# All four pairs of batch 0 with fp32 scores, two heads as row tiles of one step

## The chip, the cores and the metric

The kernel runs on one core of a Trainium2 chip. The metric is the device time of one execution in microseconds (us). Five engines work side by side, each through its own instruction list in order: TensorE (PE, matrix products; its weight loads are shown as PEld), VectorE (DVE), ScalarE (ACT), GpSimd (POOL) and SyncE (SP), which issues the DMAs here. They wait for each other through semaphores.

## The reference

Rotary attention over q, k and v of shape 4 x 8 x 576 x 64 (batch, heads, sequence, head dimension) and then an MLP over all 2304 tokens, everything in fp32:

```
q_rot, k_rot = rotate(q), rotate(k)          # x1*cos - x2*sin, x1*sin + x2*cos
scores = q_rot @ k_rot^T / sqrt(64)
attn = exp(scores - max); attn = attn / (sum(attn) + 1e-9)
x = (attn @ v) as (2304, 512)
h = x @ w_in                                 # 512 x 2048
g = s * relu(h)**2 + b
out = g @ w_out                              # 2048 x 512
```

## The kernel before

The 32 heads are 16 pairs; pairs 0 to 3 are batch 0. A pair's 2 x 576 query rows are nine score tiles of 128 rows by 576 keys: tiles 0, 1, 4, 5 belong to the first head and 2, 3, 6, 7 to the second, and tile 8 holds the last 64 rows of both heads, one above the other. Each tile runs through TensorE (`s_tile`, into one of two score buffers of two PSUM banks each), VectorE (`s_max`: scale and row minimum, in place, L652), ScalarE (`s_exp`, L388) and a normalisation that writes p as two f16 parts (`p_a`, `p_b`, into one of five buffers `pab`), then a transposing DMA (L710) and the product with v (`pv_sum`, L731).

Scores come in two ways. The pairs in `FQ`, (0, 1) here, keep q and k in fp32: after the rotation `qk_T` transposes both on TensorE by products with the identity (L739 and L742), `qk_ev` copies the result to SBUF, and `s_tile` multiplies over the 64 rows of one head (L633 and L634, in the profile each fp32 product is two passes). All other pairs split q and k into two f16 parts (`qk_hi`, `qk_lo` into `nat`), transpose them by DMA (L592), keep a copy of k with its halves swapped (`swap_k`, L601), and `s_tile` makes four f16 products over 128 rows per tile (L645 and L646). For these pairs, among the first four, `x_gram` also makes products of q and k with themselves (L537), which give the scale of the split.

Beside the attention of batch 0 the weights are loaded, rebuilt from their two words (`w_sign`, `w_low`, `w_rebias`, `w_join`), squared for their scale (`w_gram`, L456) and, for the first 256 tokens of batch 0 ("unit 0"), used in fp32 (`mlp_in0` L880, `mlp_out0` L897). All later units use weights and activations in two f16 parts (L854, L921).

No loop sets the order of the work: `plan()` lists all pieces with what they read and write, and three tables written out by hand order give the rest. `ORDER` is the order in which the pieces are issued, two letters a piece, `PICKS` the engine of each piece that can run on more than one, and `SLOTS` the buffer that each piece takes. Buffer counts are in `BUFS`. All DMAs go out on SP's queue in the order of `ORDER`.

Of the kernel before, what the change touches and what calls it, by code (L numbers as in the profile page):

```python
# [33 lines left out]
BUFS = {"s": 2, "bank": 2, "po": 1, "nat": 1, "ot": 1, "xc": 4, "xt": 1, "hr": 2, "k": 2, "q": 2, "v": 4, "z": 2, "p": 4, "pab": 5, "pt": 2, "x": 4,  # L34
        "xa": 2, "g": 3, "v16": 4, "qkT": 4, "kS": 4, "vS": 7, "dg": 2}
# [3 lines left out]
    "DTDUAAEAADD_EBEDDcDdDeDfDgAFEODhEPAEAGAHDiECELDjEEDkDlEFA3AJALEMENAIJ1EGEHEIEJEKA4AKA6J2A9DrAdDqAMA5A7DpEREQESETANAeEUJt"  # L39
    "JuJvAgAfDsDtD1AOAPDuD2DVDWDvDwJ3AQATJ4DxDXEaBAAhD3A-ARDYDZJ5DyEbA_EXJwASBBAWEcEeEdJxEmDzEfAwAyDaEgEhD0DbEpAYAxEnAzDmA0Ei"  # L40
    "AXEqD6EVAqArEWE2EjAUD7AZAaErEkElEoD4D5BCJ_KRA8KAJyAtD8EyE1BEAjDnE4KBEsKSBDKTAsEuJ6BHE5AVJzKZAbA1AmJ0LPEtEvAuJ7BGKaKCAlKb"
    "FDAkFEDoLQBRAnBSBFFABIKDAvA2J8KHAoBUAiBTEwKIBXKcBZBVBaKEKJKFD9BrBYKKBtExApD-BsFFBuKLBJKjEzBxBzKdBvBbKMKGBKFQFPBeKUKVKkAc"
    "KeB0ByBNBMKlKNB1BLLRKmBOLSKnE0KOLTKoJ9FSJ-FTK9KrBhBgKpK-KsLUKtKqKuKWKPBkBlFBBfLVBiBPLZBmK_KQBnKvBQLaFdBoFCKXK1BwB2BWBcEY"
    "E3KwKYLALbB4B7KfCSB-FrB6B5B3K2LcBdE6K3FeBpLHBjLzB8FfKgKhKxLdCUCVL0CBBqK4LIB_LJKyLeCTCAc3CCCLACLfLBLKK5CMCWLLABLWLMClLhKz"
    "LiL1LCCNKiLNLDK0L9B9bmbnblboCDCYCmLjCOK6MlCoLkL-CPCbCnL_FuK7LlLmCpMAEZCELnL2L3MBMmFRLOCsLXMJbpCabqCtCvCyLoLgMnLYc4c5Mobr"
    "E7MKMGCzE8c6E9c7E-MpC0L4C1E_CZCcc8MLL5C2MCc9FICuFGC_bwLrLpbyCFLqDCDALsFaMDCwMHbvMIc-FbCXbxbzMMCdFJCeLtLuDBbsMXCGMNFHDDLv"
    "MRb0K8LEb7b5LFb8MUCfGEGFLGCiCILwCHMYLxMSCgMVFpGHFsMZMWMOMPCJGRChCjL6Lyb6btMxL7MuMqb9b-FUCKCQMaFcMbMyMvCRDML8DNMcDPMdMzDO"
    "DQcPCxC3C4F0C5C6MrGSMQDGMwGIM0MfDJcObuNNNOCkCqNkc_cRcQb1b2NlNPCrMgDIC8C7DHMFMeMEMTMhFVM_dAC9NQF1FWFXNRM1NAFYNmFKcScTM5NS"
    "NTFZM8b3MiM2M6M9M3F2NBdBM-FMNCNnNoNpFgb4NZC-DEcUb_MtFNMsdCNDNqNEFiNHMkMjDFDKNrFhNFNaNWcVcWcADRcXdDNbNXNIFOFjN-DLcDNYNcdE"
    "M7M4GDNGNJNdN_NeNfDSdFGGNsNvcFOBcENhGOOCNtNiGPNwODOANKN1cGOMGQNLFqFmNMFtcHFkFLN2ONdGN3cIN4OOOENjNuNgFnNxNUNVcBcbcCFvOPcY"  # L50
    "dHOFFwN5OQOJOKFxN6N7FydIOGORcacJcZOrOdddOSFzF3F4F5cccdF6OecKdeOHFoF7OTOsdJOfNydfOgcecfcgOhNzGAF8dKGTdgFlGfOXN0OiOjF9OUGi"
    "dLGJOuGKdhGLdiHTOIN9OLGeGdGBcLciclckcMcjOvOkOoOVOWN8dMOpOYOtOlOwOxGhO7cmcndNOmO-dOOyOZdPF-chcocpOaO8O_dQGrO2O3GCGsPAHWO9"
    "OzPBdRdSPCGMO0PMPJObOcGNeKdTPDPNPKPLGUGWPOGgcseLcvcucteMeNGVeOdUePeQPPG5F_O4O1OqOnPZQVeReScweTdVcxGaPQPRPGGoGXeUPEPUdWQW"
    "dXdYGpGtPVdZcqcrcyegeVefQXQYeheiejeWczGYG3daPadbPSGqdcPcO5PbeXeYPdc0djekO6eZcNPedkeaPHdlPfPgGbG6PWeqGjGkc1Pnepc2dmPkdnPq"
    "GlPldoG4PIGZPFdperG7esPhQZPTPoGmHCGnPrdqHFGcPpG8QadrPsdseceeemebe-e9P6edPtetPuPie_fAdtP3ezPXelene0QbdudvP7P4euPvPwdwGwGu"
    "PyP5PYP8dxP9e1fBe2PzGvP-dyPmPjP0HRPxQIQFeofRevexfCdzQGe3QHHGQJd0e4P_QCQKQeG9G-G_ewfSeyQLd1QAQDHAQMQfd2HBHHe6Qhe5P1QQfTQN"
    "d3Qid4fUQgQjQse8QvQRQOd5HUQkQBQPQEQSHcd6d7QtQwQud8Qxd9QlGxd-fHfIfERGe7QyQzRHQpd_fJfKQ0P2fGRJfDfFQTGyQqeAHDRKRIQ3Q9fceBQm"
    "Q4QURLHKfLHtHSHVQcQrQ5fVHEeCRMQnfMeDRUfNfOfPfQHLQ-HfRNQ1Q_HIfoRORXRYeERRQdHsQoQ2GzfWHdHeRZfbRVfpfqHJfrRSfXfYRxfZfdfeHvRW"
    "fffsftfufvfwRPfxeFSNRARaRBSORbfgeGQ6fhfaRCRcSPfySQRDSRRyRfRdQ8Q7HMRzG0RufifkHXf0eIeHHYHgHZHaHbHiRTIFIIRFRQR8fzf1f2eJReRE"
    "R9RvRgRhSSRwSTR0f3f4R1fjf9gHfmR-R5R2flgIf-H5R3HjH6R6gJgKf5R_SASZHhf_gASBSCgBSagCSDSbSHSERigRf6Rlf8IQRmR4G1Hkf7gDSWgEgSRn"  # L60
    "gLRkRjSIHlSXSYIGSJHrRoSFRpScSdHogMRqR7RrIRgTIJRsSGRtHNgUgVgbS4SnSoSpSeS5H7gWISShITSfgFgNgGgcSkgmgPgXHugdSlH2SiS6geS1glSK"
    "gOG2SmSqSrS2gZTGgfgnSvgoHwS3S7SMSsH3ggSwgQgYgagigkHxgpgqgsTHH4TITTTDghgjSLHmSUSVSxSjHyStS8IHSgSuHzH0S9H1IUH-ICTAH8gwTETF"
    "TJgvgxgyTUTWSyIVH_H9TKS-TVg5gzTLTMIAfnI5HnS_IgIDHpIBSzIKhGg0HOS0TOTBTCguThTig6g7g8TjhHhIhJhKhLhMhNhOhPhQgrgtg1g2g4Tkg3g9"
    "TXTYg-hSTPTlTmI8TZhRILIMINIOIPIWIYg_hAUChbJETahThUhVUDIETbTcJFIjTeItTnhchChBhdT0hlhmhETfToTpTNhWIhTQHPheUEhfhgT_hDUAhFhn"
    "hoUBHQIuTshphqT1Tqh6TRTST2h5TxhYhXTyIXTtIZTzT3JGhZhhhjhaUSTdI7TgTrTuI6h7h8Ifh9T4T5hrUPUTUQT8UFUGT6T9UHUKUUURUIhwhthiUVUL"
    "UWTvUgUhIiUiHqTwI9hkUdhvUeUfhxhyhzhsUtiEVEhuiDUMT7UJT-JVUXIkIqUjIvh-UuUYIrUkUviFUaUlh0JHVFUoVVVWUmUpUbVGI-UwUNh1h2h4U5iG"
    "h3VXJYiHUOJIUxUyiIiOVvVwiNh_VYVxUZUcUqUnU6UzVZVaVbIsU7iPiQiAU2iCIlImU3IniBVHUriRU4iSVIU8U9U-iJVsiLIoIpU_UsikilVBIaiTiKiM"
    "iViUiYiXiminVCioipIwIyiqirisitIxIziuVJVKVLVMiZiaIbVDU1JTJUVtVuVyVPVQVNVei6iwiWVhi5ibJWVAU0icivieigVRVOVfViJXVgVjVkVlVpid"
    "ifixVziyJJVqV3V0i7i8V9WlVSV-ihiiV_izVmV4WAi0VTjEi9jDi2WJWmVnWBWnV1jFWoi4WKVUIcJeI0V5VcVrWCVdWLWDjNWXjOi-i1WUjAjCi3WpVojG"
    "jYjXi_jHI1IdV2WYjPWZjQjRWVWWjSWaWbWGWHjIWqWrJhJiJjWcjZjaWdIeW_V6XAWIV7V8WMXBjBjJI_WxjKjMjUWuJAWNWOWPWfWeWEWgWvWQWFWhjWjr"  # L70
    "WRWyWwW8WzW0jbWSJBJCWTW9W-jsXWjLjtJDjcW1W5W6JfXCjuXDXXXEJMJKjvjwW2jhXNjTXOXHXIXYWiWjXZXaXbjejVjiXcW3XPXQJgJNJLXFjjjkWkYM"
    "jdYPjljmjgj2j1jfWsXJW7WtXGW4I2I3YNXdXRYQYRXhXeXfXij3j4YOXkjojnjpXKjqJZjyYSXlJQXmXSYTXTYUYVYXJaJbj5XLkCJRJOj6JcJdXnYBkDjx"
    "jzj7j0j8j-j9kEkFkGkHkIkJkKkLkMkhkiXoJkXMXpXqkOX-ijXgXVXjXUJPJmkNJqJrJlJnkjkkXrYCXsXvXtXwXukAklYDkmX_I4YAYEYFYJkXkPkQkYkZ"
    "kRXxYdX1XykaYKYeX2YGYHj_X3YfkSXzJoYIJpkBJSkbYgYhYLYWlKY0ZtY1YYkcX4X0kUZuX5kskWYZY2ZvX6krYpYiX7X9X8ktkukTY3kVkdkekgkokflJ"
    "Y4kvY5Y6YjYqYrZwYmlLY7Y_ZAkwY8JsYnYoY9YaknkqZxYslMYtZBYlY-ZyYcYuYxYyYvYkYwlAZOZzYzZ0Z4kyZcZdZek_lBkpkxZPZQZ5lCk0ZRZfk1k2"
    "ZSkzlNZTlDlEZUYbZVk3k4ZgZZZaZhk5ZWlOZXZCZFk6ZilUk8k-lGlTZ-k7lIlQk9lFlHlPZjZGZDZEZkZlZnZHZYZoZIZbZmZJZKZplVlWlXZLZMZNZqZ_"
    "lYlRbVbWlZZrlglhlSaAZsbXodlalcZ7lbbYoeliljlklllmlnlolplqlslrofogohoiojZ8Z9aBokolltlul_mAl2aZl1leaCaGbZldmBlvlwlxlzZ1mCmK"
    "lyaHmDl3l4bamEl5l6l0l8mTmJmLl7l-mGmMmNbbmOaDaEommUl9mVacmImQmFmHmdbcadmWmXmYmSmamemPmcaaaemnmRmomZmbaIaFZ2Z3Z6lfaOabafag"
    "mfmgahaiaLmymxakalonaPmpmhmimjaQmqmrmsaJa3aMaNaRaKamajasmkopoomlmtmmataSaWaXaTaYaUaVoqaumzm0m1apmvo9mumwm2bdaqaravawa0be"
    "m4m6m3m5a4orosota5bKo8o-o_pAoyozm7pBm8axayo0o1o2pGa6ouo3anpHovoxo5a7a8a9a-a_pIa1bAbCaobDo7pQpDowbBa2azbEbLbMpJpKpLpFo4o6"  # L80
    "pCpRpEbHbgpMpNbFpSbIpTpUbJbNbObPbQbhm9pVpabGbSbTbfbRbUbipbpkplpOpWpPpXpYpcpdpepmpnpfpgbjpZpopvbkm-m_ppnAnBnCnDnEnFnGnHnI"
    "phpupwpxpypzpjprpipqnJptpsp0p2p1nKnUp3nLp5nMnNp4p6ndnTnOnVnWnXnYnenQnfn8nSngnhninPnnnonpnqnancnRnZnbnjnlnkn7nmn9nrnsn-nx"
    "n_nuntnynzn0n1oPn2nvoFnwoGoHn3oAn5n4oQoIoJoKoBn6oDoLoCoEoMoRoSoToUoOoNoWoVoXoYoaoZocob"
)

PICKS = (
    "GSSGSSGSSVSSVSSVSSVGSVSSGGSGSSGVSGGSVSGGSSVSSGGSGSSVGSGSSVGSVVSVSSGGSGSSGGSVSGVSGGSSVGSGSSVSSGSGVVSSSVVSSSVVSSSVVGGSVVSS"
    "SVVSSSVGSGGVVGGSVVSSSVVSSGGVGGGVVSSGVVVSVVVSGGVVSGGVGSGSSSSSSSSSSSSSSSSSSSVVSSGSVSSVSGSGSGSVSGSSSSSGSVSSVSSSSVSGSGSGSSSS"
    "VSSSVSSSSVSSSGVSSSSSSSVVSSSSSSSGSSSSGSSSVVSSSVSVVSSSVVSSVGSSVSGSSSGSGGVGSVGGVSGSVVVGSSSSVGSVVVGGSVSSVVSGSSSGSVSSSGSSGSGS"
    "SGSSSSGVSVSGGSVSVGVVGSGVSVVGVVSSVGVSGSSGVVVVVGVVSVVSVVSVSSSSSSSSSSVSSSGGSGGSSGSSGSSSSSSSGSSSVSVVVSGSGSGSGSGSSGSVSVSGSVSG"  # L90
    "SVSVVSVVGSVSGSVSGSVSGSSVSVSGVVVVVGSGSGVSGSGSGVGSVVVSVSGVVGSVVGVVSGSVVGVVVSVVVSGVVVVSGSGSVVVGSGVVVVSGVVSGVG"
)
# [952 lines left out]
```

## Time and profile before

| | us |
|---|---|
| median of 3 runs | 633.89 (629.41 to 634.84) |
| the profiled execution | 634.96 |
| its span | 633.2 |
| busy: TensorE | 598.2 (94%) |
| busy: VectorE | 474.5 (75%) |
| busy: ScalarE | 408.3 (64%) |
| busy: GpSimd | 133.7 (21%) |

Busy shares are means over the whole span. A TensorE row counts the time from the start of a product to its modelled end, so products that run into each other make a row's mean longer than the time from one to the next; the time from start to start in the timeline is the price of an operation. The clock that TensorE was granted is one of two levels, 1.2 or 2.4 GHz, and the profile gives it as a share of the upper one.

### The profile page before, as it was taken

What the parts mean: (1) busy time and instruction counts of PE and PEld (TensorE: products, weight loads), DVE (VectorE), ACT (ScalarE), POOL (GpSimd) and SP (SyncE); (2) the same over time, 40 slices, a digit from 0 to 9 for tenths busy, and PEclk for the clock granted to TensorE, in tenths of its full rate; (3) what the DMA queues carried; (4) which work ended last, traced back from release to release, by engine and by line L of the source; (5) the groups of instructions that cost most, each with busy time, mean ns of one, the idle gap of its engine ahead of it and who ended that gap; (6) DMA issues with size and microseconds to landing.
All of it is one profiled execution on the core that took longest, in us unless ns stands there. A gap on an engine that the chain in (4) does not pass through costs nothing.

```text
span 633.2 us, 12460 instructions
## 1 busy us (share of the span) xinstructions
PE 598.2 (94%) x4670; PEld 400.4 (63%) x4670; DVE 474.5 (75%) x1024; ACT 408.3 (64%) x855; POOL 133.7 (21%) x141
## 2 busy tenths in 40 slices
...
GB/s 284 284 239 282 170 211 175 233 137 200 210 191 147 113 153 182 142 162 173 186 170 147 134 161 121 100 197 139 146 118 72 20 89 77 20 144 21 34 2 33
DMA packets 214860, 92.09 MB, mean 145 GB/s; under 512 B 197008, under 2 KB 201232, under 8 KB 214800
## 3 DMA queue, kind: packets, MB, share of 16 engines
...
## 4 chain that ended last, share of the span: by engine, by line
PE 81%; DMA 6%; DVE 6%; ACT 4%; issue 1%; SPq 1%; DVEq 0%; ACTq 0%
PE px L854 26%; PE po L921 26%; PE px L731 8%; PE s L645 8%; PE po L897 3%; PE px L880 3%; DMA pt<-pab 2%; PE s L633 2%; DMA x<-in_moe_w_out_dram 2%; DVE wio L385 1%; PE s L646 1%; DMA x<-in_moe_w_in_dram 1%; ACT x L388 1%; DVE s L652 1%; ACT p L388 1%
## 5 line engine op out<-in xcount | busy, mean ns | idle before, releaser
L921 PE MATMUL po<-wio,g 128*128 128x512 f16 x768 | 184.3, 380 | 0.0
L854 PE MATMUL px<-xa,wio 128*128 128x256 f16 x1536 | 182.0, 273 | 0.0
L854 PEld LDWEIGHTS <-wio 128*128 128x128 f16 x1536 | 147.6, 98 | 33.5 <-issue 3.4
L388 ACT ACTIVATE p<-s,nm 128x576 f32<-128x576 f32 x144 | 105.7, 735 | 75.6 <-DVE s L652 53.0
L652 DVE TENSOR_SCALAR_CACHE_REDUCE s<-s,sc 128x576 f32<-128x576 f32 x126 | 101.6, 819 | 38.5 <-PE s L646 38.1
L385 DVE SCALAR_TENSOR_TENSOR pab<-p,sum,pab 128x576 f16<-128x576 f32 x136 | 113.6, 848 | 9.3 <-POOL pab L382 5.1
L921 PEld LDWEIGHTS <-g 128*128 128x128 f16 x768 | 70.8, 98 | 73.0 <-issue 2.8
L388 ACT ACTIVATE hr<-px,xc 128x512 f32<-128x512 f32 x64 | 43.7, 682 | 75.0 <-PE px L854 74.9
L872 POOL TENSOR_TENSOR g<-hr,g 128x512 f16<-128x512 f32 x33 | 40.6, 1230 | 194.3 <-ACT g L388 120.2
L382 POOL TENSOR_SCALAR pab<-p,sum 128x576 f16<-128x576 f32 x41 | 34.2, 836 | 139.6 <-DVE sum L680 100.8
L731 PE MATMUL px<-pt,v 128*64 128x320 f16 (+2 forms) x640 | 50.4, 283 | 5.3 <-DMA pt<-pab 2.7
L388 ACT ACTIVATE pab<-p,sum 128x576 f16<-128x576 f32 x65 | 48.4, 764 | 6.1 <-DVE sum L680 3.2
L645 PE MATMUL s<-qkT 128*128 128x512 f16 (+1 forms) x140 | 49.4, 390 | 1.0 <-ACT p L388 1.0
L645 PE MATMUL s<-kS,qkT 128*128 128x512 f16 (+1 forms) x140 | 49.2, 387 | 0.0
L645 PEld LDWEIGHTS <-qkT 128*128 128x128 f16 (+1 forms) x280 | 26.0, 101 | 30.8 <-issue 9.1
L731 PEld LDWEIGHTS <-v 128*64 128x64 f16 x640 | 33.3, 110 | 17.9 <-issue 9.9
L388 ACT ACTIVATE hr<-hr 128x512 f32<-128x512 f32 x68 | 42.6, 627 | 1.6
L756 DVE CAST g<-hr 128x512 f16<-128x512 f32 x20 | 9.4, 471 | 36.9 <-ACT hr L388 24.2
L880 PE MATMUL px<-x,wio 128*128 128x128 f32 x256 | 34.0, 285 | 0.0
L880 PEld LDWEIGHTS px<-x,wio 128*128 128x128 f32 x256 | 31.2, 196 | 3.1 <-issue 1.7
L382 POOL TENSOR_SCALAR wio<-x 128x512 bf16<-128x512 f32 (+1 forms) x26 | 22.9, 885 | 47.5 <-ACT x L388 25.5
L646 PEld LDWEIGHTS <-qkT 128*128 128x128 f16 (+1 forms) x280 | 26.0, 101 | 8.4 <-issue 2.6
...
## 6 DMA issues: line engine op xcount, KB each, us to landing
...
```

What stands on the lines that cost most here:

```text
L382: eng.tensor_scalar(out=out, in0=in0, scalar1=s1, scalar2=s2, op0=op0, op1=op1)
L385: nc.vector.scalar_tensor_tensor(out=out, in0=in0, scalar=scalar, in1=in1, op0=op0, op1=op1)
L388: nc.scalar.activation(out=out, in_=in_, func=func, **kw)
L645: nc.tensor.matmul(ps[rows, MAIN:2 * MAIN], lhs, kk[:, 4 * h:4 * h + 4], start=(n == 0), stop=(n == 1))
L646: nc.tensor.matmul(ps[rows, MAIN - TAIL:MAIN], lhs, kk[:, 8, 64 * h:64 * h + 64], start=(n == 0), stop=(n == 1))
L652: nc.vector.tensor_scalar(out=T["s"], in0=T["s"], scalar1=-1.0 / 8.0 if pr in FQ else st[pr]["es"], scalar2=None, op0=ALU.mult, op1=ALU.mi ...
L731: nc.tensor.matmul(o[64 * h:64 * h + 64, c], v_rows(pr, h, k, z), p_rows(pr, 2 * (i // 4) + h)[:, k, c], start=((z, k) == todo[0]), stop=( ...
L854: nc.tensor.matmul(ph, w16[0][:, f, wz, cc], X["xa"][:, xz, c], start=(c == 0 and n == 0), stop=(c == NC - 1 and n == 2))
L872: (nc.vector if eng == DVE else nc.gpsimd).tensor_tensor(out=g[:, 1], in0=r, in1=g[:, 0], op=ALU.subtract)
L880: nc.tensor.matmul(ph, wi[:, f + 1, c * P:(c + 1) * P], xs[0]["x"][:, c, j * P:(j + 1) * P], start=(c == 0), stop=(c == NC - 1))
L897: nc.tensor.matmul(X["po"][:, j * DM:(j + 1) * DM], gs["h", j, f - f % 4][:, f % 4 * P:(f % 4 + 1) * P], wo[:, f + 1], start=(n == 1), sto ...
L921: nc.tensor.matmul(po, g[:, gz, jj], w16[1][:, f, wz], start=(n == 1 and i == 0), stop=(n == NF and i == 2))
```

## The change

`FQ` becomes (0, 1, 2, 3): pairs 2 and 3 go the fp32 way too. A new piece `s_pair` replaces two fp32 `s_tile` pieces: the same 128 rows of both heads in one step, into both score buffers, the first head on rows 0 to 63 of the array and the second on rows 64 to 127. So that the two heads of a block stand side by side, the row order of q and k in HBM and of the rotary table changes, and `qk_T` makes one transposition of 128 x 128 in TensorE's transposing mode in place of two products of 64 columns. `pab` gets a sixth buffer, and `vS` five in place of seven. `ORDER`, `PICKS` and `SLOTS` are all new.

```diff
-FQ = (0, 1)
+FQ = (0, 1, 2, 3)
-BUFS = {... "pab": 5, ... "vS": 7, "dg": 2}
+BUFS = {... "pab": 6, ... "vS": 5, "dg": 2}
 ...
-    "DTDUAAEAADD_EBEDDcDdDeDfDgAFEODhEPAEAGAHDiECELDjEEDkDlEFA3AJ...
+    "AJDTAAEBDUAMAKALECDcDdEDDeEEDfEFEGDgANDhAdEAELEMENDiA3ADA5Af...
 ...
-        add(PE, "s_tile", *c, r=[("qkT", pr)] + ([] if F else [("kS", pr)]), w=[("s", c)])
+        if not F or i == 8:
+            add(PE, "s_tile", *c, r=[("qkT", pr)] + ([] if F else [("kS", pr)]), w=[("s", c)])
+        elif i % 4 < 2:
+            add(PE, "s_pair", *c, r=[("qkT", pr)], w=[("s", c), ("s", (pr, i + 2))])
 ...
+    def s_pair(pr, i):
+        d, t = st[pr], 2 * (i // 4) + i % 2
+        ps = [s_new(pr, i + 2 * h) for h in range(2)]
+        for to, keys in ((slice(MAIN, 2 * MAIN), slice(0, MAIN)), (slice(MAIN - TAIL, MAIN), slice(MAIN, S))):
+            for h in range(2):
+                hh = slice(64 * h, 64 * h + 64)
+                nc.tensor.matmul(ps[h][:, to], d["qF"][hh, t * P:(t + 1) * P], d["kF"][hh, keys], start=True, stop=True)
 ...
-            todo = [(h, qT[:, 4 * h + t], slice(0, P))]
+            todo = [(h, qT[:, 2 * t + h], slice(0, P))]
 ...
-                nc.tensor.matmul(ps[rows, MAIN:2 * MAIN], lhs, kk[:, 4 * h:4 * h + 4], start=(n == 0), stop=(n == 1))
+                nc.tensor.matmul(ps[rows, MAIN:2 * MAIN], lhs, kk[:, h:8:2], start=(n == 0), stop=(n == 1))
 ...
         for t in range(4):
-            for h in range(2):
-                nc.tensor.matmul(o[64 * h:64 * h + 64, t * P:(t + 1) * P], x[:, 4 * h + t], ident, start=True, stop=True)
+            nc.tensor.transpose(o[:, t * P:(t + 1) * P], x[:, 2 * t:2 * t + 2].rearrange("p h d -> p (h d)"), ident)
```

Two places show how the tables move the work. The first is TensorE about the fourth score step: `s` is a score buffer, `po` and `dg` belong to a transposition of p, `wio` to a weight's square. Before:

```order
182 L633 MATMUL s_472<-qkT_367 128x512 [waits Activation_49]
183 L634 MATMUL s_472<-qkT_367 128x64
184 L767 MATMUL po<-dg_438,p_268 128x128 [waits Activation_49]
185 L767 MATMUL po<-dg_438,p_268 128x128 x3
186 L769 MATMUL po<-dg_438,p_268 64x128 x2
187 L456 LDWEIGHTS wio [waits DVE_49]
```

and in the change:

```order
178 L776 MATMUL po<-dg_529,p_421 128x128 [waits Activation_49]
179 L776 MATMUL po<-dg_529,p_421 128x128 x3
180 L778 MATMUL po<-dg_529,p_421 64x128 x2
181 L638 MATMUL s_567<-qkT_334 128x512 [waits Activation_49]
182 L638 MATMUL s_568<-qkT_334 128x512 [waits Activation_49]
183 L638 MATMUL s_567<-qkT_334 128x64
184 L638 MATMUL s_568<-qkT_334 128x64
185 L795 MATMUL px_581<-pt_434,st_v_231 64x128 [waits DVE_49]
```

One head's two products have become the four products of two heads, and the second head's first product has a wait for ScalarE of its own, in front of both heads' 64-column products.

The second is VectorE about two maxima of neighbouring score tiles (`nm`). Before, with the second parts of pair 2's split q and k (`nat`) behind them:

```order
63 L652 TENSOR_SCALAR s_392,nm_404<-s_392 128x576
64 L652 TENSOR_SCALAR s_395,nm_430<-s_395,sc 128x576
65 L459 TENSOR_REDUCE wmx<-px_387 128x1
66 L385 SCALAR_TENSOR_TENSOR nat<-st_k_277,sc,nat 128x9x64
67 L385 SCALAR_TENSOR_TENSOR nat<-st_q_290,sc,nat 128x9x64
68 L385 SCALAR_TENSOR_TENSOR wio<-x_357,wio 128x512
```

and in the change:

```order
76 L662 TENSOR_SCALAR s_502,nm_512<-s_502 128x576
77 L383 TENSOR_SCALAR dg_536<-ident,sum 128x128
78 L388 SCALAR_TENSOR_TENSOR wio<-x_460,wio 128x512
79 L575 TENSOR_TENSOR st_k_398<-st_k_398,tab 128x576
80 L383 TENSOR_SCALAR wio<-x_517 128x512
81 L388 SCALAR_TENSOR_TENSOR v_359<-st_v_231,sc,v_359 128x640
82 L388 SCALAR_TENSOR_TENSOR wio<-x_507,wio 128x512
83 L388 SCALAR_TENSOR_TENSOR wio<-x_462,wio 128x512
84 L662 TENSOR_SCALAR s_568,nm_575<-s_568 128x576
```

The `nat` pieces of pairs 2 and 3 are gone, and weight, rotation and v pieces stand between the second maximum of one step and the first of the next.

## Rows read from the trace of the kernel before

**Rows 1.** The page: busy us (share of the span) xinstructions of each engine.
```profile
PE 598.2 (94%) x4670; PEld 400.4 (63%) x4670; DVE 474.5 (75%) x1024; ACT 408.3 (64%) x855; POOL 133.7 (21%) x141
```

**Rows 2.** Stretches: busy us per engine (instructions), granted clock, DMA share, GB/s.
```profile
25.00:50.00 25.00, 20.01 (x126) 13.70 (x125) 22.98 (x53) 19.45 (x41) 4.98 (x7) 0.61 0.92 254
...
75.00:100.00 25.00, 21.95 (x169) 14.77 (x169) 19.47 (x56) 19.26 (x43) 6.15 (x9) 0.85 0.78 181
...
175.00:200.00 25.00, 25.00 (x195) 17.01 (x194) 24.73 (x52) 22.22 (x47) 5.02 (x7) 1.00 0.76 164
...
250.00:300.00 50.00, 49.30 (x402) 32.65 (x398) 46.22 (x96) 37.18 (x82) 10.45 (x11) 1.00 0.77 159
```

**Rows 3.** TensorE's waits: line, releaser, us in total, times, longest.
```profile
PE s L633 <- ACT p L388: 2.0, 1, 2.0
PE s L645 <- ACT p L388: 1.0, 1, 1.0
```

**Rows 4.** Timeline of TensorE, 26 to 34 us: start, length, operation, count.
```profile
26.48 0.73 PE L537 MATMUL px<-st_k 128*128 128x128 bf16 x5
...
31.62 1.97 PE L739 MATMUL s<-ident,st_q 128*64 128x128 f32 x16
33.52 0.48 PE L742 MATMUL s<-ident,st_q 64*64 64x64 f32 x4
33.93 1.97 PE L739 MATMUL s<-ident,st_k 128*64 128x128 f32 x16
```

**Rows 5.** Timeline of TensorE, 80 to 92 us.
```profile
82.75 1.07 PE L633 MATMUL s<-qkT 64*64 64x512 f32 x4
83.61 0.33 PE L634 MATMUL s<-qkT 64*64 64x64 f32 x4
83.87 0.41 PE L456 MATMUL px<-wio 128*128 128x128 bf16 x4
84.11 3.79 PE L880 MATMUL px<-x,wio 128*128 128x128 f32 x32
...
91.32 0.47 PE L731 MATMUL px<-pt,v 128*64 128x128 f16 x10 [2.07 <-DVE s L652]
```

**Rows 6.** Timeline of TensorE, 124 to 131 us.
```profile
124.13 0.38 PE L645 MATMUL s<-qkT 128*128 128x512 f16 x1
...
124.62 2.03 PE L880 MATMUL px<-x,wio 128*128 128x128 f32 x16
...
128.30 1.12 PE L633 MATMUL s<-qkT 64*128 64x512 f32 x2
129.26 0.33 PE L634 MATMUL s<-qkT 64*128 64x64 f32 x2
129.43 1.07 PE L633 MATMUL s<-qkT 64*128 64x512 f32 x2
```

**Rows 7.** Groups of VectorE by form: count, busy us, mean ns, idle before.
```profile
L652 DVE TENSOR_SCALAR_CACHE_REDUCE s<-s 128x576 f32<-128x576 f32 x18 | 13.6, 758 | 2.0 <-PE s L634 2.0
...
L385 DVE SCALAR_TENSOR_TENSOR nat<-st_k,sc,nat 128x576 f16<-128x576 f32 x14 | 11.3, 809 | 0.0
...
L380 DVE TENSOR_SCALAR wio<-x 128x512 uint16<-128x512 uint16 x17 | 8.3, 489 | 1.4 <-DMA x<-in_moe_w_out_dram 1.2 <-ACT x L388 0.2
```

**Rows 8.** Groups of ScalarE by form.
```profile
L388 ACT ACTIVATE p<-s,nm 128x576 f32<-128x576 f32 x144 | 105.7, 735 | 75.6 <-DVE s L652 53.0 <-DVE pab L385 9.4 <-PE po L769 4.2
L388 ACT ACTIVATE pab<-p,sum 128x576 f16<-128x576 f32 x65 | 48.4, 764 | 6.1 <-DVE sum L680 3.2 <-ACT p L388 1.3 <-DMA pt<-pab 1.0
...
L388 ACT ACTIVATION_READ_ACCUMULATOR p<-s,nm 128x1 f32 x144 | 27.9, 194 | 0.0
...
L388 ACT ACTIVATE qkT<-s 128x576 f32<-128x576 f32 x4 | 2.6, 645 | 3.3 <-PE s L742 3.3
```

**Rows 9.** SP's waits, as rows 3.
```profile
SPq L416 <- DVE wio L385: 32.4, 14, 5.5
SPq L710 <- PE px L731: 31.3, 13, 4.7
```

151 lines of the change are left out of this document (74 added, 77 removed).

## The prediction

> **What bounds the kernel now.** I read the page first: TensorE is busy for 598.2 of 633.2 us, VectorE for 474.5 [rows 1]. The mean hides two stages, so the stretches come next [rows 2]. From 175 us on TensorE has no gap to speak of (25.00 of 25, 49.30 of 50) at the full clock: there each microsecond taken from its list is a microsecond of the time, provided the others keep up, and VectorE with 24.73 of 25 and 46.22 of 50 hardly could be faster. In the first 100 us it is otherwise: TensorE works 20.01 of 25 us at a mean clock of 0.61 (of 2.4 GHz) between 25 and 50 us and 21.95 at 0.85 between 75 and 100, while VectorE has 22.98 and 19.47 and the DMA engines 0.92 and 0.78. There TensorE waits for rotated q and k, rebuilt weights and loads; VectorE is the busiest. So the change is to be priced twice: on TensorE, where work leaves the full stage, and on VectorE, which sets how early that stage begins.
>
> **TensorE, part by part.** The timeline gives prices from start to start.
>
> - A fp32 tile of one head: 128.30 to 129.43, 1.13 us [rows 6]. Sixteen of them (pairs 0 and 1) go: -18.1 us.
> - A tile in two f16 parts: 124.13 to 124.62, 0.49 us [rows 6]. Eighteen (pairs 2 and 3) go: -8.8 us.
> - The squares of q and k of pairs 2 and 3, four groups of five: 0.73 us a group [rows 4]: -2.9 us.
> - Sixteen pair steps come. The trace has none on 64 rows by 128 columns, so both ends: one head's time, 1.13, if the two heads run side by side, or 2.26 if one follows the other. The nearest row is the fp32 tile 8, whose two heads stand on different rows and different columns: four passes of 512 and four of 64 take 82.75 to 83.87, 1.12 us for both heads [rows 5], as much as one head alone. I take 1.13: +18.1 us (above: +36.2).
> - Two more fp32 tiles 8 in place of f16 ones: 2 x 1.12 = +2.2 us.
> - `qk_T` now costs 31.62 to 33.93, 2.31 us, of which the two 64-column products are 33.52 to 33.93, 0.41 us, in the stretch with the clock at 0.61 [rows 2, 4]; four of them, 9.2 us. After, eight with four transpositions each. The transposing mode is not in the trace. From below a block costs as much as one bf16 product of 128 columns, 83.87 to 84.11 for four, 0.06 us; from above two fp32 passes of 3.79 / 32 = 0.118 us, so 0.237 us [rows 5], both at the full clock and twice that at the lower. I take one fp32 pass, being the same elements read once: 4 x 0.236 + 0.41 = 1.36 us, eight make 10.9: +1.7 us (between 8 x 0.89 = 7.1, that is -2.1, and 8 x 2.3 = 18.4, that is +9.2).
>
> Sum: -18.1 - 8.8 - 2.9 + 18.1 + 2.2 + 1.7 = -7.8 us. How much of it is on the path? Unit 0's first product, at 84.11 us [rows 5], is a mark that both orders have. Behind it stood eight of the sixteen single-head tiles, one fp32 tile 8 and eleven f16 tiles of pairs 2 and 3; behind it now stand nine of the sixteen pair steps and three tiles 8. That is -8 x 1.13 - 1.12 - 11 x 0.49 + 9 x 1.13 + 3 x 1.12 = -2.0 us, in the stage nearly without gaps, and counts in full. The other -5.8 us lies in the front, where TensorE waits for others, and is worth only what VectorE gives back too.
>
> **VectorE, ScalarE, GpSimd, SP.** Four `qk_lo` pieces go, 4 x 0.809 = -3.2 us [rows 7]. Of the passes on a weight's 16-bit halves (sign and low together) VectorE keeps 14 of 17: -3 x 0.489 = -1.5 us [rows 7]; GpSimd takes seven more sign passes and six fewer low ones, and at 21% [rows 1] covers that; without this cover `w_join`, and SP's load behind it, would wait. So VectorE's front shrinks by 4.7 us, TensorE's by 5.8. Later it takes five more `pab` casts, which costs nothing once TensorE alone is the bound. ScalarE gets four more `qk_ev` of 0.645 us, +2.6, against two `qk_hi` fewer, and ten more `pab` casts of 0.764 against eleven weight casts fewer [rows 8]: nothing, at 64%. Each pair step puts two maxima of 0.758 us [rows 7] in VectorE's list and two exponentials of 0.735 + 0.194 [rows 8] in ScalarE's, as the two tiles did before.
>
> SP loses two transposing DMAs and four `swap_k` copies. Its weight loads wait for VectorE's `w_join`, 32.4 us in 14 waits [rows 9], so a freer queue alone brings nothing; how early loads come hangs on VectorE. The sixth `pab` buffer can remove at most the 1.0 us that ScalarE's cast waited for a DMA [rows 8]: taken as 0. Two `vS` buffers fewer let `swap_v`, and the loads behind it on SP, wait for an older `pv_sum`; SP's waits for those products, 31.3 us in 13 of up to 4.7 [rows 9], cost TensorE nothing now: taken as 0, at the other end one more such wait, 4.7. The strided keys of the other pairs' products read as many columns: 0.
>
> The front is worth the smaller of the two, 4.7 us, and I take it whole, since the loads, the third party there, wait for VectorE themselves [rows 9]. Together -2.0 - 4.7 = -6.7 us. The sum is made against the profiled execution, 634.96 us (its span of 633.2 and 1.8 around it), 1.1 above the median of 633.89: **628.3 us**.
>
> **The order of passes.** What tile 8 shows [rows 5] is this: although the first head's 64-column product stands between the two heads' 512-column ones in the program, both heads end in one head's time, so the second head's passes begin before the first head's last ones. The Trainium skill, TensorE: Matmul & The Clock Gate (Part 3, "What overlaps and what doesn't"), says that products start and end strictly in program order; the trace disagrees with it for tile 8, with 1.12 us for two heads where one takes 1.13, but tile 8 parts the columns too. If program order held for pair steps, only the first head's second pass and the second head's first would overlap: three passes of 512 instead of two. Two passes take 128.30 to 129.26, 0.96 us [rows 6], one 0.48; 16 x 0.48 = 7.7 us more, 636 us.
>
> **The rivals.**
>
> 1. *Two free buffers at once (slower).* A step claims both score buffers, and the second head's product waits for the exponential of the later of the two tiles before it. If TensorE comes to a step when only the first buffer is free, the second head starts one exponential, 0.735 + 0.194 = 0.93 us [rows 8], later and the overlap is lost; the 64-column products and everything behind stand too. 16 x 0.93 = 14.9 us: 643 us. It decides from 6.7 / 16 = 0.4 us a step. For it: almost every second product has such a wait, and a step leaves both buffers without work for VectorE while it runs. Against it: now TensorE waits for the exponentials only 2.0 and 1.0 us in all [rows 3], and the order puts 4 to 5 us of other VectorE pieces between two steps. 0.15.
> 2. *VectorE takes the gain back.* From 175 to 300 us it is at 24.73 of 25 and 46.22 of 50 [rows 2], and over the whole program its load hardly falls: -3.2 - 1.5, and five `pab` casts and other pieces come back. If TensorE arrives earlier only to wait for it, some 5 us return: 634 us. Against it: in that stretch TensorE, too, has no gap, so the two are level. 0.13.
> 3. *Program order of passes*, or some other half overlap: 636 us. 0.07.
> 4. *The front closes up (faster).* Between 75 and 100 us the lower clock costs 0.15 x 21.95 = 3.3 us [rows 2], and behind tile 8 TensorE stands 2.07 us before 91.32 for a maximum [rows 5]. If the shorter front has no such gap and the clock stays up, another 5.4 us go, with some of the 25 to 50 us stretch (0.39 x 20.01 = 7.8 us lost there) 8: 621 us. The order is new throughout, so the gaps will not be the same ones. 0.15.
>
> The forecast itself, 624 to 633 us, has 0.50.
>
> **Numbers.** About 1% is what a measurement of this kernel can tell from no change: 627.55 and 640.2 us about the median. Below 627.55 lie rival 4 and a bit under half of the forecast's own spread, 0.23: faster 0.38. Above 640.2 lies rival 1: slower 0.15. The rest, 0.47, is within 1%. The range for 8 in 10 reaches from 618 (rival 4 with blocks transposed at the lower price) to 640; it leaves out most of rival 1 and the far end of rival 4.
>
> **What would show it.** In the changed kernel's timeline a pair step in full clock from its first product to the next operation: 1.1 to 1.2 us is right, 1.6 is rival 3, 2 and more with a wait for ScalarE in it rival 1. `qk_T`: 1.4 us at the lower clock. TensorE's busy time should fall by 6 to 8 us, and unit 0's first product should stand some 5 us before 84.11. Were VectorE named in new waits of TensorE between 175 and 300 us, rival 2 holds; were the clock full from 70 us on, rival 4. Wrong in any case: a front that lengthens because the first loads now begin with a weight ahead of k and the table.

## The result and the profile after

The changed kernel takes 627.42 us (median of 20 runs, 624.03 to 630.37), the kernel before 633.94 us on the same chip (20 runs, 627.46 to 635.25): a ratio of 0.9909, interval 0.9888 to 0.993. It is 5.8 us faster by the ratio; the sum had 6.7 us and 628.3 us. The profiled execution took 627.53 us, its span 625.7.

The page, busy time and TensorE's clock in 40 slices (tenths of the upper level), answers to [rows 1]:

```profile
PE 588.8 (94%) x4634; PEld 396.5 (63%) x4634; DVE 470.6 (75%) x1029; ACT 407.3 (65%) x858; POOL 123.8 (20%) x127
PEclk9987999999999999999999999999999999999999
```

TensorE is busy for 9.4 us less, VectorE for 3.9 us less. The stretches answer to [rows 2], in the same columns:

```profile
25.00:50.00 25.00, 19.25 (x130) 13.86 (x129) 18.95 (x47) 20.58 (x42) 9.26 (x13) 0.85 0.78 264
75.00:100.00 25.00, 23.69 (x243) 18.02 (x243) 23.14 (x61) 22.42 (x52) 8.59 (x9) 1.00 0.99 251
175.00:200.00 25.00, 25.00 (x190) 16.73 (x189) 24.87 (x51) 22.70 (x46) 2.79 (x4) 1.00 0.63 139
250.00:300.00 50.00, 48.66 (x389) 31.94 (x387) 43.39 (x91) 40.50 (x85) 9.81 (x8) 1.00 0.87 173
```

The stage from 175 us on is as full as it was. Between 75 and 100 us the clock is higher, 1.00 against 0.85, and TensorE, VectorE and the DMA engines all have little left. The 0.85 between 25 and 50 us can't be held against the older 0.61 as it stands: this trace has no record of the clock before 32.4 us and counts it as 1.00 there, although the rows up to then have the lengths of the lower level (below, `qk_T` takes 1.43 us at 27.31; at 40.96 one takes 0.86). With the lower level up to 32.4 us the stretch comes to about 0.70, an estimate; the older trace has its first record at 13.9 us. TensorE's waits (line, releaser, us, times, longest) answer to [rows 3]; the first three lines are the longest of the whole span, the others one for VectorE's rotation and the one for exponentials at score tiles:

```profile
PE px L540 <- DMA st_v<-in_v_dram: 9.4, 2, 8.8
PE px L741 <- DMA pt<-pab: 6.7, 8, 1.5
PE s L748 <- ACT p L391: 3.6, 1, 3.6
...
PE s L748 <- DVE st_q L577: 1.3, 1, 1.3
...
PE s L645 <- ACT p L391: 1.1, 2, 0.8
```

The first line is in the main the program's first load (8.76 us). The transposing DMA of p is waited for eight times. Between 175 and 300 us it is the only thing that TensorE waits for, 1.3 us in two waits; VectorE is not named there. The third line is new: `qk_T` writes into a score buffer, and until 23.93 us it waits for an exponential of the first pair step's tiles, 3.6 us; in the kernel before no `qk_T` waits for ScalarE.

The timeline of TensorE (start, length, operation, count) shows the two new operations. First `qk_T`, where [rows 4] had it:

```profile
27.31 1.09 PE L748 MATMUL s<-ident,st_q 128*128 128x128 f32 x4
28.33 0.48 PE L751 MATMUL s<-ident,st_q 64*64 64x64 f32 x4
28.74 1.11 PE L748 MATMUL s<-ident,st_q 128*128 128x128 f32 x4
```

From 27.31 to 28.74 one takes 1.43 us; 1.36 was estimated for the lower clock. Then pair steps, the last of them at full clock:

```profile
15.71 2.40 PE L638 MATMUL s<-qkT 64*128 64x512 f32 x8 [0.26 <-ACT qkT L391]
...
47.20 3.21 PE L638 MATMUL s<-qkT 64*128 64x512 f32 x8
50.34 0.61 PE L459 MATMUL px<-wio 128*128 128x128 bf16 x4
...
66.77 1.30 PE L638 MATMUL s<-qkT 64*128 64x512 f32 x8
68.00 1.46 PE L795 MATMUL px<-pt,st_v 128*64 128x128 f32 x20
```

From 66.77 to 68.00 a step of two heads takes 1.23 us, where one head alone took 1.13 [rows 6]. Eleven of the sixteen steps take this 1.23; one takes about 1.4 and one 1.5 (at 59.62), and the other three, at 15.71, 47.20 and 53.32, take 2.40 (to its own end), 3.14 and 2.48 (to the next start). The last two lie in the stretch from 42.6 to 56.2 us with the granted clock at its lower level; the one at 15.71 stands before the first record of the clock. That is 24.5 us for sixteen, against 18.1.

The marks: unit 0's first product (L889) and unit 1's first product (L863):

```profile
78.79 3.84 PE L889 MATMUL px<-x,wio 128*128 128x128 f32 x32
...
178.08 2.14 PE L863 MATMUL px<-xa,wio 128*128 128x256 f16 x18
```

Before they stood at 84.11 [rows 5] and, in the same view:

```profile
188.33 1.92 PE L854 MATMUL px<-xa,wio 128*128 128x256 f16 x15
```

TensorE is 5.3 us ahead at the first mark, 10.3 us at the second, and 7.5 us at the end of the span. VectorE's groups by form (count, busy us, mean ns, idle) answer to [rows 7], ScalarE's last one to [rows 8]:

```profile
L662 DVE TENSOR_SCALAR_CACHE_REDUCE s<-s 128x576 f32<-128x576 f32 x36 | 26.8, 766 | 6.1 <-PE s L638 6.1
L388 DVE SCALAR_TENSOR_TENSOR nat<-st_k,sc,nat 128x576 f16<-128x576 f32 x12 | 10.2, 848 | 0.0
...
L383 DVE TENSOR_SCALAR wio<-x 128x512 uint16<-128x512 uint16 x14 | 6.5, 494 | 4.4 <-DMA x<-in_moe_w_in_dram 3.1 <-DMA x<-in_moe_w_out_dram 1.3
L391 ACT ACTIVATE qkT<-s 128x576 f32<-128x576 f32 x8 | 5.0, 639 | 3.9 <-PE s L751 3.9
```

The counts are the forecast's: two `nat` pieces fewer in this group and two in the other, 14 weight passes for 17, eight copies of the transposed q and k.

### The profile page after: what moved, and what is told of

Same layout as the page of the kernel before. It is cut to its first block, busy times and chain, and to the rows that moved or that the text cites. A ratio compares the mean times of both kernels' runs of the same rounds, so it can differ in the third digit from the quotient of the medians.

```text
span 625.7 us, 12358 instructions
## 1 busy us (share of the span) xinstructions
PE 588.8 (94%) x4634; PEld 396.5 (63%) x4634; DVE 470.6 (75%) x1029; ACT 407.3 (65%) x858; POOL 123.8 (20%) x127
## 4 chain that ended last, share of the span: by engine, by line
PE 73%; DMA 10%; DVE 7%; ACT 3%; issue 3%; SPq 2%; POOL 1%; DVEq 0%; ACTq 0%; POOLq 0%
PE px L863 25%; PE po L930 24%; PE px L741 8%; PE s L656 7%; DMA pt<-pab 5%; PE po L906 2%; PE px L889 2%; PE s L638 2%; DVE s L662 2%; DMA x<-in_moe_w_in_dram 2%; DMA x<-in_moe_w_out_dram 2%; DVE wio L388 1%; DMA qkT<-nat 1%; PE s L657 1%; ACT x L391 1%
## 5 line engine op out<-in xcount | busy, mean ns | idle before, releaser
L863 PE MATMUL px<-xa,wio 128*128 128x256 f16 x1536 | 181.8, 273 | 0.0
L863 PEld LDWEIGHTS <-wio 128*128 128x128 f16 x1536 | 148.3, 98 | 32.8 <-issue 1.3
L662 DVE TENSOR_SCALAR_CACHE_REDUCE s<-s,sc 128x576 f32<-128x576 f32 x108 | 87.7, 820 | 24.7 <-PE s L657 22.3
L881 POOL TENSOR_TENSOR g<-hr,g 128x512 f16<-128x512 f32 x31 | 39.0, 1257 | 189.5 <-ACT g L391 100.2
L391 ACT ACTIVATE pab<-p,sum 128x576 f16<-128x576 f32 x75 | 56.2, 766 | 9.8 <-DVE sum L690 8.0
L385 POOL TENSOR_SCALAR pab<-p,sum 128x576 f16<-128x576 f32 x26 | 23.4, 902 | 123.2 <-DVE sum L690 70.4
L741 PEld LDWEIGHTS <-v 128*64 128x64 f16 x640 | 35.6, 109 | 18.7 <-issue 13.0
L656 PE MATMUL s<-qkT 128*128 128x512 f16 (+1 forms) x120 | 41.4, 383 | 0.0
L656 PE MATMUL s<-kS,qkT 128*128 128x512 f16 (+1 forms) x120 | 41.3, 380 | 0.0
L656 PEld LDWEIGHTS <-qkT 128*128 128x128 f16 (+1 forms) x240 | 21.9, 100 | 25.1 <-issue 5.0
L889 PE MATMUL px<-x,wio 128*128 128x128 f32 x256 | 32.3, 279 | 0.0
L889 PEld LDWEIGHTS px<-x,wio 128*128 128x128 f32 x256 | 30.0, 192 | 3.1 <-issue 2.2
L662 DVE TENSOR_SCALAR_CACHE_REDUCE s<-s 128x576 f32<-128x576 f32 x36 | 26.8, 766 | 6.1 <-PE s L638 6.1
```

The lines of the kernel that those rows point to most:

```text
L385: eng.tensor_scalar(out=out, in0=in0, scalar1=s1, scalar2=s2, op0=op0, op1=op1)
L391: nc.scalar.activation(out=out, in_=in_, func=func, **kw)
L656: nc.tensor.matmul(ps[rows, MAIN:2 * MAIN], lhs, kk[:, h:8:2], start=(n == 0), stop=(n == 1))
L662: nc.vector.tensor_scalar(out=T["s"], in0=T["s"], scalar1=-1.0 / 8.0 if pr in FQ else st[pr]["es"], scalar2=None, op0=ALU.mult, op1=ALU.mi ...
L741: nc.tensor.matmul(o[64 * h:64 * h + 64, c], v_rows(pr, h, k, z), p_rows(pr, 2 * (i // 4) + h)[:, k, c], start=((z, k) == todo[0]), stop=( ...
L863: nc.tensor.matmul(ph, w16[0][:, f, wz, cc], X["xa"][:, xz, c], start=(c == 0 and n == 0), stop=(c == NC - 1 and n == 2))
```

## The experiments

Below, a cost against the changed kernel is the difference of the two ratios to the kernel before, times 634 us, with the two intervals combined as independent ones; for kernels built on the one before it is the ratio itself. It is good to about 2.5 us. The runs come in three groups, each with 29 to 34 runs of the kernel before beside it and none of the changed kernel.

**1. Both heads on the same rows.** The pair step, its waits and its order stay; the second head's operands are the first's, so its scores are the first head's.

```diff
-                hh = slice(64 * h, 64 * h + 64)
+                hh = slice(0, 64)
```

> The changed kernel with one edit: both heads of a pair step take rows 0 to 63 (the second head's scores are then the first's, so it computes something else), so the two heads can only follow each other; order, waits and all else as they were. Theory A (the pair step runs both heads side by side, and what it saves on TensorE is on the path behind unit 0's first product): a step rises from the 1.23 us of the changed kernel's timeline to about 2.1 us at the full clock; nine steps behind the first product of unit 0 cost 9 x 0.9 = 8 us in full and the seven in front some part of 6 us: 636 to 641 us. Rival B (the gain came from the new order and the clock, the length of the step is hidden): 626 to 630 us.

635.58 us, ratio 1.0041 (1.0006 to 1.0076): 8.4 us more, the whole gain of 5.8 and something besides. The timeline of TensorE at the step that the changed kernel has at 66.77:

```profile
65.92 2.37 PE L638 MATMUL s<-qkT 64*128 64x512 f32 x8
68.23 0.40 PE L459 MATMUL px<-wio 128*128 128x128 bf16 x4
```

2.31 us for 1.23: on the same rows one head follows the other, on different rows they run side by side. Sixteen steps are 17 us longer at the full clock, and about half of that reaches the end. Nine of them stand behind unit 0's first product, 9.7 us; that the other seven fall into gaps of the front is likely, but not shown.

**2. Products in place of the transposing mode.**

```diff
-            nc.tensor.transpose(o[:, t * P:(t + 1) * P], x[:, 2 * t:2 * t + 2]..., ident)
+            for h in range(2):
+                nc.tensor.matmul(o[64 * h:64 * h + 64, t * P:(t + 1) * P], x[:, 2 * t + h], ident, ...)
```

> The changed kernel with the transpositions of q and k made by two products of 64 columns again, eight per piece in place of four in the transposing mode. Each of the eight pieces should go from 1.43 us back to 2.31 us at the lower clock: 7 us more on TensorE, all in the first 48 us. Theory A (VectorE and loads set the front, TensorE has gaps there): 628 to 631 us. Rival B (TensorE sets the front): 633 to 635 us.

627.56 us, ratio 0.9918 (0.9885 to 0.995): 0.6 us, nothing. In its timeline a `qk_T` is longer:

```profile
29.55 1.76 PE L749 MATMUL s<-ident,st_q 128*64 128x128 f32 x16
31.23 0.33 PE L752 MATMUL s<-ident,st_q 64*64 64x64 f32 x4
31.50 0.41 PE L459 MATMUL px<-wio 128*128 128x128 bf16 x4
```

1.95 us for 1.43. The eight pieces take 16.1 us in place of 11.0, all before 47 us, and these 5 us cost nothing: there TensorE is not the bound.

**3. The row order and the transposing mode alone, on the kernel before.** `FQ`, the tables and the single-head tiles stay as they were.

```diff
-                nc.tensor.matmul(o[64 * h:64 * h + 64, t * P:(t + 1) * P], x[:, 4 * h + t], ident, ...)
+            nc.tensor.transpose(o[:, t * P:(t + 1) * P], x[:, 2 * t:2 * t + 2]..., ident)
...
-                ... kk[:, 4 * h:4 * h + 4] ...
+                ... kk[:, h:8:2] ...
```

> The kernel before with the new row order of q, k and the rotary table and the transposing mode alone: four pieces of transposed q and k at about 1.43 in place of 2.31 us, and the other fourteen pairs' score products read keys with a stride. Theory A (front under VectorE, strided keys free): 631 to 634 us. Rival B (the transposing mode carries the gain): below 630 us. Rival C (strided keys slow the f16 score products): above 636 us, and the time from one f16 score tile to the next product above 0.49 us.

634.27 us, ratio 1.0035 (0.9995 to 1.0076): no gain. By themselves these two parts of the change bring nothing, and the strided keys cost no more than the interval leaves; in this trace an f16 tile still takes 0.48 to 0.50 us to the next product (114.69 to 115.17, 124.24 to 124.74).

**4. VectorE's load raised: eight passes, then four.** In the first, each of the eight copied q and k (pairs 0 to 3) gets one more pass over its 128 x 576 values on VectorE (the values are doubled), some 6.4 us; in the second only those of pairs 2 and 3, some 3.2 us, what the four `qk_lo` pieces had been.

```diff
         copy(eng, f, d.pop(("T", nm))[:, 0:576])
+        nc.vector.tensor_tensor(out=d[nm], in0=d[nm], in1=d[nm], op=ALU.add)   # second: if pr >= 2
```

> The changed kernel with one VectorE pass of 128x576 fp32 more behind each of the eight copies of transposed q or k (it doubles a tile that nobody reads again), about 8 x 0.8 = 6.4 us more on VectorE in the first 60 us, nothing more on any other engine. Theory A (VectorE sets how early the full stage begins): 632 to 635 us, first product of unit 0 some 5 us later. Rival B (loads or single waits set the front, VectorE has room): 627 to 629 us.

> The changed kernel with one more VectorE pass over the transposed q and k of pairs 2 and 3 each (four passes of about 0.8 us, some 3.2 us, the amount of the four qk_lo pieces that the change removed; it doubles those values). Theory A (VectorE's removed work is a term of the gain, about one for one): 629.5 to 631.5. Theory B (slack in front of these pairs; the eight passes of e3 hurt by the first two pairs, which come first): 626 to 628. Theory C (more than one for one, as in e3): 631 to 633.

Eight passes: 636.27 us, ratio 1.0061 (1.003 to 1.0091), 9.6 us more (7.3 to 12.0) and above every range named. Four passes: 631.02 us, ratio 0.9993 (0.9961 to 1.0025), 5.3 us more (2.9 to 7.8); one for one, 3.2, is inside its interval, nothing is not. The mark of unit 0's first product, with eight and with four:

```profile
85.68 3.84 PE L890 MATMUL px<-x,wio 128*128 128x128 f32 x32
```

```profile
83.11 3.84 PE L891 MATMUL px<-x,wio 128*128 128x128 f32 x32
```

It moves 6.9 and 4.3 us back from 78.79 (the profiled execution with four passes took 636.00 us, the longest of its twelve).

The runs do more than load VectorE, though. The added pass writes the buffer of the loaded q or k, and the next load into that buffer waits for it on SP, with the loads of weights behind it. SP's longest waits ahead of loads of q, k and v (L511), in the changed kernel and then with eight and with four passes:

```profile
SPq L511 <- PE s L751: 7.7, 3, 4.5
```

```profile
SPq L511 <- DVE st_k L760: 18.3, 2, 9.7
```

```profile
SPq L511 <- DVE st_k L761: 8.4, 1, 8.4
```

The load of k that goes out at 25.50 us in the changed kernel goes out at 30.37 and 28.11, and VectorE itself waits for loads of q and k, 2.4 and 2.3 us, where it had no such wait. The pages have VectorE busy for 7.5 and 3.2 us more (478.1 and 473.8 for 470.6); with these waits that is 9.9 and 5.5, against 9.6 and 5.3 at the end. So more work on VectorE in the front comes out at the end, but its load and the later buffers were not told apart.

**5. VectorE's load lowered in the front: the changed kernel, then the kernel before.** The last pass of the rotation is left out for the first four pairs (the rotation is incomplete), eight passes, 6.4 us.

```diff
-        eng.tensor_tensor(out=x, in0=x, in1=z, op=ALU.add)
+        if pr >= 4:
+            eng.tensor_tensor(out=x, in0=x, in1=z, op=ALU.add)
```

> The changed kernel without the last of three VectorE passes of the rotation of q and k of the first four pairs (eight passes of about 0.8 us less on VectorE; the rotation of these pairs is left incomplete). Theory A (VectorE sets the front, one for one or a bit more, as the 8.8 us for eight passes more say): 619 to 622 us. Rival B (below its present load VectorE no longer decides, loads do): 624 to 627 us.

> The kernel before, but the last of the three passes of rotate is left out for q and k of the first four pairs (eight passes of about 0.8 us, nearly all on VectorE, in the first 100 us; their rotation stays incomplete). It is the mirror of e7 on the older kernel. Theory A (the forecast's VectorE term): the front of the kernel before is set by VectorE, so 6.4 us less on it give 4 to 6 us: 628 to 630. Theory B (VectorE does not decide in the front of either kernel; what the changed kernel gained came from TensorE's own list and the clock there): 632 to 635. Theory C (gained in front and given back further on): unit 0's first product some 4 us earlier than 84.11, but the end within 2 us of the kernel before.

On the changed kernel: 625.97 us, ratio 0.9919 (0.9886 to 0.9951), 0.6 us against it by the ratios, no gain; its page has VectorE busy for only 3.9 us less (466.7 for 470.6), so the other pieces took longer. On the kernel before: 628.48 us, ratio 0.9932 (0.9895 to 0.9969), 4.3 us less (2.0 to 6.7), with VectorE busy for 7.2 us less (467.3 for 474.5). So the older kernel's front hung on VectorE, or on what stands behind this pass: the transposition of q and k and with it the buffer of their next load. The pass left out brings three quarters of what the whole change brings. In the changed kernel it brings nothing, so something else ends its front. In the changed kernel with less VectorE these are TensorE's longest waits in the first 180 us:

```profile
PE px L540 <- DMA st_v<-in_v_dram: 8.9, 1, 8.9
PE px L742 <- DMA pt<-pab: 5.3, 6, 1.5
PE po L777 <- ACT pt L391: 3.1, 2, 2.2
PE s L639 <- ACT qkT L391: 2.6, 2, 2.2
PE s L749 <- ACT p L391: 2.4, 1, 2.4
```

The first is the program's first load. Behind it come transposing DMAs of p and then ScalarE, three times, ahead of any piece of VectorE. Which of them ends the changed kernel's front was not tried: no run took a transfer or a piece of ScalarE away.

**6. VectorE's load lowered behind the front.** The same pass is left out where VectorE does it for pairs 4 to 15: 21 passes, some 16 us by their lengths, of which 10.8 show in VectorE's busy time (459.8 for 470.6).

```diff
+        if pr < 4 or e != DVE:
             eng.tensor_tensor(out=x, in0=x, in1=z, op=ALU.add)
```

> The changed kernel, but the last pass of rotate is left out where VectorE does it for pairs 4 to 15 (rotation incomplete): some 20 passes of 0.75 to 0.8 us less on VectorE, 16 us in all, ten of them (7.5 us) between 175 and 300 us. The front of the first four pairs is as in the changed kernel. Rival 2 (VectorE takes part of the gain back after the front): 622 to 625, and the stretch from unit 1's first product to the end, 447.6 us in the changed kernel, falls to 443 to 445. Forecast (TensorE alone is the bound there, whatever VectorE does): 626 to 629, 447 to 448 us.

626.9 us, ratio 0.9916 (0.9883 to 0.9949): 0.4 us, nothing. Its stretch from 250 to 300 us, to be held against the changed kernel's above:

```profile
250.00:300.00 50.00, 48.15 (x379) 30.97 (x377) 40.73 (x84) 39.70 (x84) 9.15 (x8) 1.00 0.85 176
```

VectorE has 2.7 us less to do and TensorE does no more for it. From unit 1's first product to the end it is 448.1 us, in the changed kernel 447.6.

**7. The order of products in the step.** The first head's 512 and 64 columns, then the second's.

```diff
-        for to, keys in ((slice(MAIN, 2 * MAIN), slice(0, MAIN)), (slice(MAIN - TAIL, MAIN), slice(MAIN, S))):
-            for h in range(2):
+        for h in range(2):
+            for to, keys in ((slice(MAIN, 2 * MAIN), slice(0, MAIN)), (slice(MAIN - TAIL, MAIN), slice(MAIN, S))):
```

> The changed kernel, but a pair step issues the first head's two products (512 and 64 columns) before the second head's two, where it alternated between the heads. Both heads still stand on their own 64 rows. Theory A (a product begins as soon as its own rows are free, whatever stands in front of it on the other rows): the pair step stays at 1.2 to 1.3 us and the time at 626 to 629. Theory B (products start in program order, so the alternation makes the overlap): the second head's first product waits until the first head's 64-column product has begun its last pass, the step takes some 1.9 to 2.1 us, 16 x 0.7 = 11 us of TensorE more, and the time is 633 to 638.

627.34 us, ratio 0.9949 (0.9916 to 0.9981): by the ratios 2.5 us more (0.1 to 5.0), at the edge of the uncertainty, and by the median the changed kernel's time. The step itself:

```profile
64.64 1.30 PE L638 MATMUL s<-qkT 64*128 64x512 f32 x8
65.88 1.46 PE L795 MATMUL px<-pt,st_v 128*64 128x128 f32 x20
```

1.24 us. The overlap needs no alternation in the program. In the records of this step the second head's first product starts 0.01 us after the first head's, at 64.66, and no product of 64 columns before 65.61, though the program has the first head's between them.

**8. The clock in the front.** On both kernels products of ones without use are put on TensorE ahead of the weights' squares and of the first `x_gram`, to keep it busy where it waits.

```diff
+    def fill(o, n):
+        for i in range(n):
+            nc.tensor.matmul(o, ones16b, ones16b, start=True, stop=True)
```

> The changed kernel with idle products added on TensorE in the front: 60 products of 128 columns (ones by ones) ahead of the first square, 8 ahead of the next ones and 10 ahead of each of the first eleven weight squares, into the same bank that the real product then overwrites; they fill waits and keep TensorE's activity up. Theory A (VectorE sets the front; the clock there is worth little): 626 to 630 us. Rival D (the lower clock in the first 60 us is what costs; in the changed kernel's profile TensorE works at half speed up to about 32 us and again from 42 to 56 us): 621 to 625 us, with pair steps at 1.23 us from the first.

> The kernel before with the same idle products: 60 ahead of the first square, 8 ahead of the other seven, 10 ahead of each of the first ten weight squares. Theory A: 632 to 636 us, no change. Rival D (the lower clock between 21 and 45, 61 and 68, and 92 and 103 us costs the kernel before some 6 us, and the change's gain is mostly a clock that falls less): 626 to 630 us.

The changed kernel: 626.04 us, ratio 0.992 (0.989 to 0.9951), no difference, though TensorE had more of the upper level: the record, which begins at 6.6 us, has the lower one for 17 us up to 34 us, and from 50 to 75 us the clock was full, where the changed kernel had 0.88 and the lower level from 42.6 to 56.2 us besides what stands before 32.4. The kernel before: 637.56 us, ratio 1.0091 (1.005 to 1.0132), slower by 5.8 us, outside both ranges, and its clock did not stay up; three of its stretches:

```profile
0.00:25.00 25.00, 16.00 (x177) 13.12 (x178) 18.30 (x34) 8.82 (x14) 4.59 (x8) 0.86 0.79 278
25.00:50.00 25.00, 19.82 (x186) 15.42 (x184) 22.02 (x49) 18.19 (x38) 5.42 (x6) 0.80 1.01 233
...
100.00:125.00 25.00, 22.90 (x161) 16.50 (x159) 17.75 (x38) 17.73 (x41) 5.95 (x8) 0.80 0.98 218
```

In the changed kernel a higher clock in the front was not seen to be worth anything; the older kernel did not get one in this way, so for it this stays open.

**9. The kernel before once more,** unchanged, for one look at how far its front varies.

> The kernel before, unchanged, profiled once more. Theory A and rival D alike: about 634 us with the clock at half in some 40 to 50 us of the first 103. Should this execution be one of the faster ones (627 to 630 us), rival D wants fewer microseconds at the lower clock in it, theory A wants an earlier first product of unit 0 at the same clock.

632.34 us. Unit 0's first product and the stretch behind it:

```profile
78.75 3.79 PE L880 MATMUL px<-x,wio 128*128 128x128 f32 x32
```

```profile
75.00:100.00 25.00, 21.34 (x159) 14.80 (x160) 16.30 (x48) 16.79 (x38) 3.52 (x5) 0.73 0.84 185
```

The mark is 5.4 us earlier than in the first profile of the same kernel and where the changed kernel has it, yet the span, 630.5 us, is only 2.7 us shorter: a longer stretch at the lower clock follows (0.73 for 0.85). A single mark in the front varies by as much as the change moves it.

The other runs of the kernel before say more. Of the 80 used for the ratios, the 23 with a mean granted clock of 0.975 or more have a median of 628.5 us, the 43 with 0.970 or less 633.3. In its quicker executions the older kernel thus comes within 1.1 us of the changed kernel's 627.42. Whether a lower clock makes the front long or a long front brings the lower clock, these runs don't show, so rival D of runs 8 and 9 stays open for the older kernel. It is not the whole of run 5: at the same clock, 0.970 to 0.979, the kernel before takes 627.8 us without the pass (median of 8) and 629.7 with it (14).

## Why the prediction held

**Pair steps.** The likelier end was right: 1.23 us at full clock against 1.13 taken and 2.26 as the other end; sixteen at 1.23 are 19.7 us, 1.6 more than the term. Run 1 shows that the separate rows make it, and that without them the gain is gone.

**Rival 1 (two free buffers at once)** came once in sixteen. In the step at 47.20 the second head's first product starts 0.82 us after the first head's, behind its wait for ScalarE, and the step takes 3.14 us where two times 1.23 would be 2.46. With the steps of about 1.4 and 1.5 some 1.1 us are drawn out beyond their clock, for 14.9 in the rival. The wait that the forecast did not price stands elsewhere: `qk_T` takes a score buffer too, and one of them waits 3.6 us for an exponential.

**Rival 3 (program order of passes)** would have shown 1.6 us a step and shows 1.23, with the alternation or without. The rule of the Trainium skill that the prediction weighed, that products start and end strictly in program order (TensorE: Matmul & The Clock Gate, Part 3, "What overlaps and what doesn't"), does not hold for fp32 products on different rows here: in run 7's order it would let only the first head's last pass and the second head's first overlap, and the step takes 1.24 us, with the second head's first product ahead of the first head's last.

**TensorE's sum.** -7.8 us was forecast, the page has -9.4. Against the second profile of the kernel before (run 9), in which the same products take 594.1 us in place of 598.2, it is -5.3: the two pages bracket the sum and can't test it more closely. One of its terms was misread: the squares' 0.73 us is a length, from start to start it is 0.51 (25.97 to 26.48), so they were worth -2.0 and not -2.9.

**`qk_T`.** 1.43 us for 1.36: the size was right and the term was worth nothing either way, as run 2 shows. The far end of that bound, +9.2 us, did not belong in a sum over the path.

**VectorE's 4.7 us, taken whole.** Runs 4 and 5 agree with this step on both kernels: four passes, as much as the removed `qk_lo`, cost 5.3 us (interval 2.9 to 7.8), and eight taken out of the older kernel give 4.3. They don't show it alone, since both also move the buffers and loads of q and k, and since the older kernel's time goes with its clock (run 9); that VectorE's load is what ended the older front is in part argued. VectorE's front also shrank by more than the term: up to unit 0's first product it is busy for 63.3 us in place of 70.3, as a maximum and other pieces moved behind the mark. The rule of "the smaller of the two" fits: less work on VectorE brings nothing in the changed kernel (run 5), and the TensorE time that run 2 adds costs nothing. What TensorE gained up to unit 1's first product is busy time, 148.6 us for 159.4, with the clock's part in it; its idle time there is nearly the same, 29.5 and 28.9.

**-2.0 us behind unit 0's first product, -4.7 in front.** The two profiles show -2.1 and -5.3 in their spans. This agreement is luck. The stretches behind the mark, the kernel before and then the changed one:

```profile
84.11:633.20 549.09, 538.49 (x4229) 357.79 (x4226) 404.15 (x871) 355.57 (x743) 110.28 (x111) 0.99 0.59 130
```

```profile
78.79:625.70 546.91, 533.38 (x4229) 357.14 (x4226) 407.28 (x887) 352.82 (x743) 103.28 (x97) 1.00 0.62 129
```

TensorE has 5.1 us less to do there, not 2.0, and 2.9 us more idle time; the older kernel ran 10.2 of these us at the lower clock, from 92.4 on. And by run 9 the kernel before, run again, has the front's mark 5.4 us earlier and gives half of it back behind it, so that against that profile the whole 4.8 us of difference lie behind the mark and none in front. What is firm is the sum, 5.8 us by the ratio against 6.7.

**Rival 2 (VectorE takes gain back)** did not come as VectorE's wait: none between 175 and 300 us, and run 6. But of the 10.3 us lead at unit 1's first product, 2.8 are gone at the end. The stretches from there to the end, the changed kernel and then the one before, show where:

```profile
178.10:625.70 447.60, 440.13 (x3498) 292.93 (x3494) 318.13 (x679) 271.94 (x565) 75.21 (x69) 1.00 0.55 114
```

```profile
188.40:633.20 444.80, 438.71 (x3489) 290.71 (x3487) 313.51 (x659) 272.69 (x563) 89.28 (x87) 1.00 0.52 115
```

TensorE has 1.4 us more work behind the mark, pieces that the new order has put there (a score tile and two products of unit 0 stand behind it now), and 1.4 us more idle time. So half of the lead's loss was never a gain.

**Rival 4 (the front closes up)** came by half: the clock between 75 and 100 us was full, its sign, and the gap of 2.07 us behind tile 8 is gone, but others came in its place and the 621 us did not follow. By run 8 the changed kernel's front gains nothing from a still higher clock. How much of the 5.8 us is the lower clock that the older kernel has behind unit 0's first product, no run shows.

**The last sign,** a front that lengthens by its first loads, shows as 0.8 us: TensorE's first product starts at 8.76 us in place of 7.99.
